# Two DRAINs on GpSimd among the scatters of an attention and mixture-of-experts kernel

## The chip, the cores and the metric

One core of a Trainium2 chip runs one program from its first instruction to its last. The metric is the time of one execution in microseconds on the device (us), taken as the median of three runs. The engines are called as in the profile: PE (TensorE), DVE (VectorE), ACT (ScalarE), POOL (GpSimd) and SP (SyncE). A name with a q behind it (POOLq, SPq) is the engine's queue, where waits on semaphores, branches and DRAINs are recorded.

## The reference, cut to what matters

```python
scores = scale * q @ k.T                        # 8 x 8 heads, 576 x 576, head_dim 64
bias = -(cum[:, :, :, None] - cum[:, :, None, :])     # cum: cumsum of max(s, 0)
scores = where(causal, -1e9, scores + minimum(bias, 0))
attn = exp(scores - max) / (sum + 1e-9)
x = (attn @ v) laid out as 4608 tokens x 512
logits = x @ w_gate + modality_bias[modality_id]      # 8 experts
e_idx = argmax(logits);  gate_w = softmax(logits)[e_idx]
for e in range(8):                              # each token goes to one expert
    h = maximum(x[e_idx == e] @ w1[e], 0)       # 512 -> 1024
    out[e_idx == e] = gate_w * (h @ w2[e])      # 1024 -> 512
```

## The kernel before, in words

The program has two stages. In the attention stage 32 pairs of heads are worked off one after the other. Finished tokens are sorted by expert: each row of a token goes to a list in device memory by an indirect DMA that POOL issues (line L724, 36 of them, of 128 tokens each at most). Besides, POOL splits the queries and keys into a high and a low part in this stage (L323, L327).

The second stage is the expert stage. `M.run` in `build` takes a list of 19 blocks. The first 18 are blocks of 256 tokens of one expert each (`block`, which ends in `second`), the nineteenth takes two quarters of 64 tokens in one go (`two`). Each block loads its tokens and its expert's weights by DMAs on SP, ACT and DVE split the weights into two parts, PE multiplies, and the scaled result `ys` is written to its rows of the output by indirect DMAs that POOL issues, here called scatters: two in each of the 18 blocks (L1067, 128 rows each, the first released by ACT at L1066, the second by DVE at L1064), one in the nineteenth (L1177, 128 rows in two halves from DVE at L1176). `M.last[2]` always holds the scatter that was issued last. From the first of these scatters on POOL has nothing else to do in this stage.

Behind the 19 blocks stands a loop over further quarters (`For_i` at L1355) with a count that is read from the routing (L1353). In the profiled execution its body does not run. Behind the loop each engine waits for the semaphores of all others (rows with L1355), and then comes the end of the program (rows with L1379): a DRAIN on each engine, a meeting of all engines through semaphores that POOL leads, the clearing of the semaphores, and a second meeting.

The order on each engine is that in which a scheduler lets the instructions go; `tc.issue_after(i)` puts the instructions made inside it behind the instruction i on their engine. `finish(k)` is called ahead of block number k, counted from zero, so at its call `M.last[2]` is the last scatter of the k-th block counted from one.

Of the kernel before, what the change touches and what calls it, by code (L numbers as in the profile page):

```python
# [1287 lines left out]
def build(tc, qkv, s, mid, wg, mb, w1, w2, out):  # L1288
    nc = tc.nc
    with ExitStack() as ctx:  # L1290
        dr = ctx.enter_context(tc.tile_pool(name="dr", bufs=1, space=DRAM))
        lists = dr.tile([8 * CAP, ROW], F32, name="lists")
        c = ctx.enter_context(tc.tile_pool(name="const", bufs=1))
        ident = c.tile([P, P], F32, name="ident")
        make_identity(nc, ident)
        R = Route(ctx, tc, lists)
        M = Moe(ctx, tc, R, w1, w2, ident, out)
        xctx = ctx.enter_context(ExitStack())
        pos = []
        with ExitStack() as actx:  # L1300
            xps = [xctx.enter_context(tc.tile_pool(name="xp0", bufs=2, side="right"))]
            A = Attn(actx, tc, qkv, s, ident, wg)

            def newx(bp):
                if bp == 1:
                    A.t1.close()
                    xps.append(xctx.enter_context(tc.tile_pool(name="xp1", bufs=2, side="right")))
                xp = xps[bp % 2]
                return [xp.tile([P, 4, XW // 2, 8, 2], F32, name="x"), xp.tile([P, 4, XW // 2, 8, 2], F32, name="x"),
                        xp.tile([P, 1, XW // 2, 8, 2], F32, name="xq", bufs=1)]  # L1310

            pos.append(lambda: A.xo)

            def done(bp, x):
                def first():
                    yield from R.first()
                    yield from M.early()
                yield from R.group(bp, x, lambda: pos[0](), A.pw_ if bp < 3 else None, (lambda: A.bg.append([first(), False])) if bp == 2 else None)

            setup = {**A.more, 5: A.consts, 14: R.consts, 17: lambda: A.save(0), 26: lambda: A.save(1), 20: lambda: R.setup(mid, mb, A.t1p)}  # L1320
            bg = A.run(32, newx, done, setup)
            assert len(bg) == 1
            for _ in range(NGS):
                next(bg[0][0])
        with ExitStack() as mctx:
            M.open(mctx)
            pos[0] = lambda: M.ps.tile([P, 512], F32, name="rt", bufs=1)

            def routed():
                with ExitStack() as after:  # L1330
                    for i in M.tr:
                        after.enter_context(tc.issue_after(i.ins))
                    after.enter_context(tc.high_priority(offset=PRI2))
                    for _ in bg[0][0]:
                        pass
                xctx.close()
                M.open2(mctx)

            def finish(k):
                if 1 <= k <= 4:  # L1340
                    with ExitStack() as after:
                        for i in (M.hold, M.last[1].ins):
                            after.enter_context(tc.issue_after(i))
                        R.pad((2 * k - 2, 2 * k - 1))
                        if k == 2:
                            for _ in R.rest():
                                pass

            M.run([("t2", b, 2) for b in range(N2)] + [("t3", b, 2) for b in range(N3)] + [("t4", 0, 0)], early=True, then=finish, routed=routed)
            with ExitStack() as after:  # L1350
                for i in [M.hold] + [i.ins for i in M.last]:
                    after.enter_context(tc.issue_after(i))
                n = nc.values_load(R.t4["tot"][0:1, 0:1], min_val=0, max_val=NQ)  # L1353
            M.stop = 1 << 30
            with tc.For_i(NS, n) as i:  # L1355
                M.hold = None
                M.run([("t4", i, 1)])
# [25 lines left out]
```

## Time and profile before

| | us |
|---|---|
| median of three runs | 837.39 (836.03 to 838.33) |
| the profiled execution | 836.2 |
| its span, first to last instruction | 834.4 |
| PE busy in the span | 812.8 (97%) |
| POOL busy in the span | 360.8 (43%) |
| last scatter (L1177) starts | 823.71 |

The span is what the trace shows; the 1.8 us between it and the execution's own time lie outside the records. The views used below are the page, the answers on one line of the kernel (for each operation on each engine: how many, the shortest, the median and the longest duration in ns, and the first and the last start in us), the timeline of POOL (start, duration, engine, line, operation, and in brackets how long the engine sat idle before and what ended that) and a table of the busy time of each engine in chosen stretches.

### The profile page before, as it was taken

How to read it: one execution, taken by the hardware profiler on the slowest of the kernel's cores; microseconds unless marked ns; L12 is line 12 of the kernel's file. 1: busy time of each engine (PE TensorE's matmuls, PEld its weight loads, DVE VectorE, ACT ScalarE, POOL GpSimd, SP SyncE). 2: the span in 40 equal slices, each digit the busy share in tenths (PEclk: the TensorE clock that was granted, in tenths of full speed). 3: DMA queues.
4: the chain of work that ended last, by engine and by line, in shares of the span. 5: the costliest groups of instructions: out<-in, count | busy, mean ns of one | idle time of the engine just before them, and what ended most of it. 6: DMA issues, size and time to landing. Idle time of an engine off the chain costs nothing. (4 is left out here: it accounts for less than half of the span.)

```text
span 834.4 us, 16877 instructions
## 1 busy us (share of the span) xinstructions
PE 812.8 (97%) x5692; PEld 696.1 (83%) x5692; DVE 545.9 (65%) x1502; ACT 541.8 (65%) x1292; POOL 360.8 (43%) x384
## 2 busy tenths in 40 slices
PE   7999999999999999999999999999999999999994
PEld 6778887887888778778988889999988889999872
DVE  6666667666766677767389766555556666555872
ACT  6888888888888888885265555544445555544662
POOL 8959768988688877991410000000000000000110
PEclk9999999999999999999999999999999999999997
DMA  7665555866667656737797866665555566665950
GB/s 234 185 195 179 180 177 185 261 206 193 178 188 227 204 164 198 230 106 268 259 375 257 310 243 255 255 251 204 205 205 205 214 250 255 255 236 208 355 181 3
DMA packets 68549, 182.31 MB, mean 218 GB/s; under 512 B 7993, under 2 KB 8889, under 8 KB 68334
## 3 DMA queue, kind: packets, MB, share of 16 engines
q1 hardware_dynamic: 62622, 161.17, 57.1%
q0 software_dynamic: 5840, 20.06, 6.2%
q8 instruction: 45, 0.74, 0.4%
q14 instruction: 42, 0.34, 0.1%
HBM read 144.73 MB, written 26.80 MB: 206 GB/s over the span
## 5 line engine op out<-in xcount | busy, mean ns | idle before, releaser
L1067 POOL DMA_INDIRECT out<-ys,oi x36 | 36.8, 1023 | 368.1 <-ACT ys L1066 297.5
L397 DVE CUSTOM_DVE_ANT_0 pe<-sp,mk 128x512 f32<-128x512 f32 (+3 forms) x256 | 121.3, 488 | 63.1 <-PE sp L395 58.9
L417 ACT ACTIVATE pe<-pe,mx 128x512 f32<-128x512 f32 (+3 forms) x256 | 143.9, 563 | 21.4 <-DVE mx L397 20.0
L427 PE MATMUL pt<-ident,pe 128*128 128x128 f32 x640 | 118.6, 283 | 3.3 <-ACT PT L430 2.3
L430 ACT COPY PT<-pt 128x512 f32<-128x512 f32 (+3 forms) x256 | 106.6, 417 | 13.7 <-PE pt L427 13.0
L1083 ACT ACTIVATE hT<-hp 128x512 fp32r<-128x512 f32 x72 | 42.9, 595 | 93.0 <-PE hp L1081 92.6
L467 PE MATMUL o<-PT,V 128*64 128x320 f32 (+4 forms) x896 | 100.7, 364 | 0.0
L373 PE MATMUL sp<-KA,QH 128*128 128x256 f32 (+2 forms) x256 | 97.1, 388 | 1.8 <-POOL KA L236 1.8
L427 PEld LDWEIGHTS pt<-ident,pe 128*128 128x128 f32 x640 | 76.0, 142 | 26.3 <-ACT PT L430 10.5
L467 PEld LDWEIGHTS o<-PT,V 128*64 128x64 f32 x896 | 58.6, 136 | 41.0 <-issue 9.2
L1081 PE MATMUL hp<-xT,wcb 128*128 128x256 f32 x648 | 89.6, 282 | 0.0
L395 PE MATMUL sp<-KB,QL 76*128 76x256 f32 (+2 forms) x256 | 88.3, 349 | 1.3 <-DMA QL<-ek 1.3
L1081 PE MATMUL hp<-xT,wca 128*128 128x256 f32 x624 | 87.3, 282 | 0.5 <-ACT xT L1033 0.5
L327 POOL TENSOR_TENSOR KA<-rawk,KA 64x576 fp32r<-64x576 f32 x62 | 86.9, 1418 | 0.2
L327 POOL TENSOR_TENSOR QL<-rawq,QH 64x576 fp32r<-64x576 f32 x62 | 86.7, 1413 | 0.2
L1084 DVE SCALAR_TENSOR_TENSOR hT<-hp,hT 128x512 fp32r<-128x512 f32 x72 | 49.5, 688 | 55.5 <-ACT hT L1083 55.5
L1081 PEld LDWEIGHTS hp<-xT,wcb 128*128 128x128 f32 x648 | 83.1, 188 | 0.6
L1081 PEld LDWEIGHTS hp<-xT,wca 128*128 128x128 f32 x624 | 80.4, 188 | 1.4 <-issue 0.7
L1056 PE MATMUL y<-wcb,hT 128*128 128x512 f32 x336 | 81.2, 398 | 0.0
L1056 PEld LDWEIGHTS y<-wcb,hT 128*128 128x128 f32 x336 | 62.8, 188 | 14.7
L1081 PE MATMUL hp<-xT,wcc 128*128 128x256 f32 x456 | 64.6, 281 | 0.0
L1056 PE MATMUL y<-wca,hT 128*128 128x512 f32 x264 | 63.9, 398 | 0.0
(285 smaller groups left out, 1614.0 us busy)
## 6 DMA issues: line engine op xcount, KB each, us to landing
wrbw<-in_w SPq DMA_DIRECT2D x104, 512.0 KB
wraw<-in_w SPq DMA_DIRECT2D x56, 512.0 KB
rawq<-in_qkv SPq DMA_DIRECT2D x31, 576.0 KB
rawk<-in_qkv SPq DMA_DIRECT2D x31, 576.0 KB
xg<-lists SPq DMA_DIRECT2D x18, 576.0 KB
V<-in_qkv SPq DMA_DIRECT2D x32, 320.0 KB
KB<-KA SPq DMA_DIRECT2D x62, 144.0 KB
lists<-z SPq DMA_DIRECT2D x8, 576.0 KB
```

What stands on the lines that cost most here:

```text
L327: self.last = nc.gpsimd.tensor_tensor(o, i, h, ALU.subtract).ins
L373: self.pe.append(self.nc.tensor.matmul(sp[:, :nn], QH[:, q0:q0 + P], self.KA[u][:, ab, :nn], start=True, stop=False).ins)
L395: self.pe.append(nc.tensor.matmul(sp[:, :nn], QL[:EXT, q0:q0 + P], KB[:EXT, ab, :nn], start=False, stop=True).ins)
L397: ins = nc.vector.tensor_tensor_reduce(out=t[:, :n], in0=sp[:, :n], in1=self.mk[:, 512 - n:512], scale=-0.125, scalar=3.0e38, op0=ALU.add, ...
L417: self.act = nc.scalar.activation(t[:, :n], t[:, :n], AF.Exp, bias=m, scale=-1.0, accum_out=st["sums"][:, o:o + 1]).ins
L427: self.pe.append(nc.tensor.transpose(out=pt[:, P * j:P * j + P], in_=pe[:, P * j:P * j + P], identity=self.ident).ins)
L430: cp(w[:, :, v:v + P], pt[:, :P * (c + 1)].rearrange("p (j q) -> p j q", q=P))
L467: m = nc.tensor.matmul(o[r, f - q0:q1 - q0], V[:, ab, j, :], PT[ab][:, PTS * j + f if j < 4 else PTW - 64:PTS * j + q1 if j < 4 else PTW], ...
L1056: self.last[0] = nc.tensor.matmul(y[u], hT[:, a, f, P * u:P * u + P], W[4 + f // 2][:, c, 512 * (f % 2):512 * (f % 2) + 512], start=f == 0 ...
L1081: nc.tensor.matmul(hp[:, u], W[k][:, a, f:f + P], xT[:, c, k], start=k == 0 and i == 0, stop=k == 3 and i == 2)
L1083: hi = nc.scalar.activation(hs, hp, AF.Relu)
L1084: lo = nc.vector.scalar_tensor_tensor(hT[:, 1, 2 * m:2 * m + 2], hp, 0.0, hs.bitcast(F32), ALU.max, ALU.subtract)
```

## The change

Two DRAIN instructions on POOL are added. The one at k = 10 stands behind the second scatter of the tenth block, the one at k = 18 behind the second scatter of the eighteenth. A DRAIN has no operands. In the built program neither of the two carries a wait on a semaphore or raises one, and nothing else waits for them. Every other instruction of all five engines keeps its place, its waits and its updates: on POOL 16 scatters lie between the two DRAINs, and the only scatter behind the second one is that of the nineteenth block (L1177).

```diff
             def finish(k):
+                if k in (10, 18):
+                    with tc.issue_after(M.last[2].ins):
+                        nc.gpsimd.drain()
                 if 1 <= k <= 4:
                     with ExitStack() as after:
                         for i in (M.hold, M.last[1].ins):
```

## The prediction

> **What bounds the kernel now.** I began with the head of the page and its chain of waits.
>
> ```profile
> span 834.4 us, 16877 instructions
> PE 812.8 (97%) x5692; PEld 696.1 (83%) x5692; DVE 545.9 (65%) x1502; ACT 541.8 (65%) x1292; POOL 360.8 (43%) x384
> ...
> POOL out L1177 0%; POOLq L1353 0%
> ```
>
> PE is busy 97% of the span, so up to the last block PE sets the time, and POOL at 43% does not. The chain of the end, however, hangs on POOL: its last piece is the scatter at L1177. So next I cut the end of the span into stretches (busy time of each engine, clock, DMA share, GB/s).
>
> ```profile
> 815.00:823.70 8.70, 6.93 (x32) 4.57 (x31) 4.24 (x7) 3.09 (x5) 0.00 (x0) 1.00 0.00 0
> 823.70:826.40 2.70, 0.00 (x0) 0.00 (x0) 0.00 (x0) 0.00 (x0) 0.98 (x1) 0.87 0.07 21
> 826.40:827.50 1.10, 0.00 (x0) 0.00 (x0) 0.00 (x0) 0.00 (x0) 0.00 (x0) 0.50 0.00 0
> 827.50:833.60 6.10, 0.00 (x0) 0.00 (x0) 0.00 (x0) 0.00 (x0) 0.00 (x0) 0.50 0.00 0
> 833.60:834.40 0.80, 0.00 (x0) 0.00 (x0) 0.00 (x0) 0.00 (x0) 0.00 (x0) 0.50 0.00 0
> ```
>
> From 823.7 on no engine computes but for one scatter of 0.98 us, and in the 6.10 us from 827.5 to 833.6 nothing is busy and no byte moves. The answer on the end's line, L1379, says what stands there.
>
> ```profile
> L1379 POOLq EVENT_SEMAPHORE  x4: 17/17/17, 833.6 to 834.3; - x4
> L1379 SPq DRAIN  x3: 7/7/13, 827.0 to 833.9; - x3
> L1379 POOLq DRAIN  x3: 45/103/6043, 827.6 to 834.2; - x3
> L1379 ACTq DRAIN  x2: 8/8/8, 827.1 to 833.9; - x2
> L1379 DVEq DRAIN  x2: 10/14/17, 827.3 to 833.9; - x2
> L1379 PEldq DRAIN  x2: 8/8/8, 827.4 to 833.9; - x2
> ```
>
> Four engines pass their first DRAIN in 7 to 17 ns. POOL's three DRAINs take 45, 103 and 6,043 ns. The long one is the first: it starts at 827.6, and POOL's next semaphore event is at 833.6. All engines wait for POOL in this meeting, so these **6.04 us lie on the path that sets the end**, one for one.
>
> **What the long DRAIN may be made of.** The only DRAIN that POOL runs earlier is in the program's head:
>
> ```profile
> L1367 POOLq DRAIN  x1: 173/173/173, 0.4 to 0.4; - x1
> ```
>
> It stands behind four memsets and takes 0.17 us. The two that follow the long one at the end take 0.10 and 0.05 us. So a DRAIN is short when POOL has issued no DMA before it or since the last DRAIN, and the only long one has all of the program's indirect DMAs behind it:
>
> ```profile
> L724 POOL DMA_INDIRECT lists<-x,di x32: 956/1064/1973, 144.0 to 404.6; - x32
> L724 POOL DMA_INDIRECT lists<-xq,di x4: 960/1025/1065, 190.1 to 405.9; - x4
> L1067 POOL DMA_INDIRECT out<-ys,oi x36: 983/983/1442, 407.1 to 810.8; - x36
> L1177 POOL DMA_INDIRECT out<-ys,oi x1: 984/984/984, 823.7 to 823.7; - x1
> DMA to landing us min/median/max: 2.6/2.6/2.6
> ```
>
> That makes 32 + 4 + 36 + 1 = 73. The last landed at 823.71 + 2.6 = 826.3, before the long DRAIN began, so it is not waiting for data. My reading is that POOL keeps something open for each DMA that it issued and settles it in the DRAIN: 6.043 us / 73 = 83 ns for each, an estimate. If so, a DRAIN leaves the next one only what was issued since.
>
> **The change part by part.** Where the two new DRAINs stand is seen in POOL's timeline.
>
> ```profile
> 618.52 0.98 POOL L1067 DMA_INDIRECT out<-ys,oi  x1 [17.98 <-ACT ys L1066]
> 623.24 0.98 POOL L1067 DMA_INDIRECT out<-ys,oi  x1 [3.73 <-DMA out<-ys,oi]
> 642.04 0.98 POOL L1067 DMA_INDIRECT out<-ys,oi  x1 [17.82 <-ACT ys L1066]
> ...
> 810.82 0.98 POOL L1067 DMA_INDIRECT out<-ys,oi  x1 [2.51 <-DMA out<-ys,oi]
> 823.71 0.98 POOL L1177 DMA_INDIRECT out<-ys,oi  x1 [11.91 <-DVEq L1355]
> ```
>
> *First DRAIN.* The tenth block's second scatter ends at 623.24 + 0.98 = 624.22; the next instruction of POOL that does anything starts at 642.04, after 17.82 us of idling, and waits for ACT. Queued behind the DRAIN are only the next scatters. By my reading it settles 36 + 20 = 56 DMAs, 56 x 83 ns = 4.6 us. Bounds: 0.05 us from the shortest DRAIN row, 6.04 us from the longest. If it has to wait for the scatter's landing as well, that adds no more than the longest landing of a scatter:
>
> ```profile
> DMA to landing us min/median/max: 2.7/5.2/7.7
> ```
>
> Even 7.7 + 6.04 = 13.7 us fit into the 17.82. Cost on the path: 0. The cover is ACT's and PE's work on the eleventh block; without it the whole length would count.
>
> *Second DRAIN.* The eighteenth block's second scatter ends at 811.80, and the last one, L1177, starts at 823.71 when DVE's `ys` is ready: 11.91 us of idling. The queue event ahead of L1177 shows when the scatter before it had landed:
>
> ```profile
> L1177 POOLq EVENT_SEMAPHORE  x1: 17/17/17, 813.6 to 813.6; - x1
> ```
>
> So the landing is through at 813.6. The DRAIN settles 16 DMAs, 16 x 83 ns = 1.3 us; at the upper bound, 6.04 us begun at 813.6, it ends at 819.6, 4.1 us ahead of need. Cost on the path: 0 at either bound, covered by PE, ACT and DVE in the nineteenth block.
>
> *Last DRAIN of the program.* One DMA is left, L1177. Lower bound 0.05 us, upper bound 6.04 us, as now. I take the sum of a short DRAIN and one DMA's share, 0.10 + 0.08, rounded to 0.2 us, since the rows for a DRAIN with little behind it (0.05, 0.10, 0.17) are nearest to that case. Gain: 6.04 - 0.2 = 5.84 us, taken as 5.8.
>
> *What else could shrink.* POOL runs one more queue instruction near the end:
>
> ```profile
> L1355 POOLq INC_SWDGE_SEM  x1: 1638/1638/1638, 824.5 to 824.5; - x1
> L1355 POOLq EVENT_SEMAPHORE  x12: 42/43/43, 826.4 to 827.3; - x12
> ```
>
> If its 1.64 us too come from open DMAs, POOL's twelve semaphore waits start sooner, but the fifth of them still has to wait for the landing at 826.3; only four of them, some 0.08 us apart, come forward. That is at most 0.4 us; I put it into the lower end of the range and not into the sum.
>
> **Sum.** Against the profiled execution: 836.2 - 5.8 = 830.4 us (span 834.4 - 5.8 = 828.6, and the same 1.8 us around it). The median of the runs lies 1.2 us above that execution, at 837.39; against it the forecast is 831.6 us, and I write 831.5.
>
> **The rivals.** *First: the 6.04 us stay, time 837.4.* The long part could belong not to the 73 but to whatever stands behind the second new DRAIN: the scatter L1177, the INC_SWDGE_SEM, or a fixed price for a DRAIN after any DMA. Then the two new ones take 6.04 us each under cover, the last takes 6.04 again, and nothing moves. For it: there is one long DRAIN in the trace, and one point cannot tell a price per DMA from a fixed one. Against it: in the head an INC_SWDGE_SEM is followed by a DRAIN of 0.17 us, and one scatter of 128 rows that has landed is little to spend 6 us on.
>
> ```profile
> L1367 POOLq INC_SWDGE_SEM  x1: 31/31/31, 0.2 to 0.2; - x1
> ```
>
> The Trainium skill, GPSIMD Engine Reference, section 2.1 Instruction dispatch, gives such a fixed price: the first call of freshly loaded code pays a load of about 6 us that no instruction shows. By that rule the time stays 837.4. The stretch 827.5 to 833.6 shows a DMA share of 0.00, so no load is seen, though it need not be recorded.
> The Trainium skill, VectorE: DVE Perf Modes, section The DRAIN you can't avoid, calls the DRAINs around a program a constant of about 12 ns on all five engines. By that rule too nothing could be won, and the time stays 837.4. The rows of four engines agree (7 to 17 ns); POOL's 6,043 ns do not.
>
> *Second: a part stays.* If half of the 6.04 is per DMA and half fixed, 3.0 us are won: 834.4. No row speaks for it beyond the same single point.
>
> *Third, on the other side: the scatter behind the second DRAIN gets dearer.* L1177 is on the chain, so each us that its 0.98 grows is a us of the end. If a DRAIN throws out what scatters keep on POOL, and fetching it costs what the long DRAIN costs, L1177 takes 7.0 us and the last DRAIN is as long as before: 837.4 + 6.0 = 843.4. It decides from 2.5 us on if the last DRAIN keeps its 6.04, and from 5.8 us on if it shrinks. Against it: the spread of all 73 issues is 0.96 to 1.97 us, though POOL does other work between them in the first stage.
>
> **How the numbers follow.** Chances: forecast 0.79, the 6.04 us stay 0.13, a part stays 0.04, the scatter gets dearer 0.04. A measurement of this kernel tells about 0.3%, 2.5 us, from no change. Forecast and part-stays are faster: 0.83; no change 0.13; slower 0.04. For the range: around 831.5 the runs of before spread by -1.4 and +0.9; below, the 0.4 us of INC_SWDGE_SEM come on top, which gives 829.7; above, I go to 834.4, the case in which a part stays. That leaves out the first and third rival, 0.17.
>
> **What would show it.** Right: the last stretch of the trace has a POOL DRAIN of under 0.5 us between the semaphores of L1355 and the meeting, the added DRAINs take about 4.6 and 1.3 us (with the landing in front), the scatters after them start at the same distance behind `ys` as now, and PE's time up to 823 is unchanged. Wrong: the DRAIN at the end is still near 6 us (first rival) or 3 us (second), or L1177 takes well over 1 us (third).

## The result, and the profile after

| | before | changed |
|---|---|---|
| median of four runs | 836.71 us (835.80 to 838.33) | 829.38 us (829.02 to 830.96) |
| the profiled execution | 836.2 us | 829.02 us |
| its span | 834.4 us | 827.3 us |
| last scatter (L1177) starts | 823.71 us | 823.07 us |
| POOL's first DRAIN at the end | 6.043 us | 0.128 us |

The changed kernel takes 0.9914 of the time of before, with a 95% interval of 0.9893 to 0.9935: it is faster, by a little under 1%. The forecast was 831.5 us with a range from 829.7 to 834.4. The sign and the mechanism are as forecast; the measured median lies 0.3 us below the range.

In the changed kernel the line of the loop's end is L1358 (L1355 before) and that of the program's end L1382 (L1379 before). The answer on the end's line (operation, count, shortest, median and longest duration in ns, first and last start in us):

```profile
L1382 POOLq EVENT_SEMAPHORE  x4: 17/17/17, 826.5 to 827.2; - x4
L1382 SPq DRAIN  x3: 7/7/13, 826.1 to 826.7; - x3
L1382 POOLq DRAIN  x3: 51/103/128, 826.2 to 827.0; - x3
```

The long DRAIN is gone: 128 ns where it took 6,043. The same answer for the line of the two added DRAINs, and for the end of the loop:

```profile
L1342 POOLq DRAIN  x2: 3655/7172/10688, 622.3 to 810.1; - x2
...
L1358 POOLq EVENT_SEMAPHORE  x12: 42/43/1122, 824.0 to 826.0; - x12
L1358 POOLq INC_SWDGE_SEM  x1: 193/193/193, 823.6 to 823.6; - x1
```

The added DRAINs took 10.69 and 3.66 us. Behind the last scatter, INC_SWDGE_SEM fell from 1,638 to 193 ns. The page's head and the stretches at the end (start and end, length, then busy time of PE, its weight loads, DVE, ACT and POOL, clock, DMA share, GB/s):

```profile
span 827.3 us, 16879 instructions
PE 812.1 (98%) x5692; PEld 695.5 (84%) x5692; DVE 545.6 (66%) x1502; ACT 541.3 (65%) x1292; POOL 360.5 (44%) x384
```

```profile
823.10:825.40 2.30, 0.00 (x0) 0.00 (x0) 0.00 (x0) 0.00 (x0) 0.95 (x1) 0.70 0.07 22
825.40:826.20 0.80, 0.00 (x0) 0.00 (x0) 0.00 (x0) 0.00 (x0) 0.00 (x0) 0.50 0.00 0
826.20:826.50 0.30, 0.00 (x0) 0.00 (x0) 0.00 (x0) 0.00 (x0) 0.00 (x0) 0.50 0.00 0
826.50:827.30 0.80, 0.00 (x0) 0.00 (x0) 0.00 (x0) 0.00 (x0) 0.00 (x0) 0.50 0.00 0
```

Each engine has as many instructions as before, but for the two DRAINs, and its busy time is the same within 0.1%; the empty stretch of 6.10 us at the end became one of 0.3 us. POOL's timeline around the added DRAINs (start, duration, engine, line, operation, idle time before and what ended it):

```profile
622.50 0.98 POOL L1067 DMA_INDIRECT out<-ys,oi  x1 [3.62 <-DVE hT L1084]
641.41 0.98 POOL L1067 DMA_INDIRECT out<-ys,oi  x1 [17.93 <-ACT ys L1066]
...
810.30 0.98 POOL L1067 DMA_INDIRECT out<-ys,oi  x1 [2.52 <-DMA out<-ys,oi]
823.07 0.98 POOL L1177 DMA_INDIRECT out<-ys,oi  x1 [11.78 <-DVEq L1358]
```

The scatters behind both DRAINs still wait for ACT and DVE, after 17.93 and 11.78 us of idling (17.82 and 11.91 before): the DRAINs lie wholly inside that idle time.

The 834.44 - 827.27 = 7.17 us between the two spans divide into pieces:

| piece of the span | before | changed | difference |
|---|---|---|---|
| start to L1177 | 823.71 | 823.07 | -0.64 |
| L1177's start to the start of POOL's first DRAIN at the end | 3.845 | 3.172 | -0.67 |
| that DRAIN | 6.043 | 0.128 | -5.92 |
| the rest (meeting of the engines) | 0.84 | 0.90 | +0.06 |

The first piece is not the change's doing. It stands in the trace by the first of the indirect DMAs to the lists, 480 us ahead of the first added DRAIN:

```profile
L724 POOL DMA_INDIRECT lists<-x,di x32: 959/1064/1973, 143.4 to 404.0; - x32
```

That is 143.4 against 144.0 before, and from there on the two traces stay about as far apart (0.5 to 0.7 us at the scatters shown). In the traces of the runs below, this first start lies anywhere from 143.4 to 146.9 whether or not a DRAIN was added, so one pair of traces cannot be compared closer than some microseconds ahead of L1177; only the pieces behind it can.

### The profile page after: what moved, and what is told of

Same layout as the page of the kernel before. It is cut to its first block, busy times and chain, and to the rows that moved or that the text cites. A ratio compares the mean times of both kernels' runs of the same rounds, so it can differ in the third digit from the quotient of the medians.

```text
span 827.3 us, 16879 instructions
## 1 busy us (share of the span) xinstructions
PE 812.1 (98%) x5692; PEld 695.5 (84%) x5692; DVE 545.6 (66%) x1502; ACT 541.3 (65%) x1292; POOL 360.5 (44%) x384
## 6 DMA issues: line engine op xcount, KB each, us to landing
KB<-KA SPq DMA_DIRECT2D x62, 144.0 KB
```

## The experiments

**Theories.** A: POOL keeps each DMA that it issued open and settles it in its next DRAIN, about 0.083 us each; the DRAIN also waits for the landing of the last scatter (the time at which the trace shows its data arrived). A DMA is called open here when POOL has issued it since its last DRAIN. B: the end's DRAIN has a fixed price (a load of some 6 us, or a price of a DRAIN after any DMA) that a DRAIN somewhere earlier pays once. C: a price per DMA that depends on what else runs, since the first added DRAIN took 10.69 us, not 4.6.

**The changed kernel once more, alone and beside the others.** No edit. It ran in two of the three series.

> The changed kernel itself, unaltered, once more. The theory of open DMAs (POOL's DRAIN settles each DMA that POOL issued since its last DRAIN; the one at the program's end shrinks from 6.04 to about 0.13 us): 0.8% faster than before, some 6.5 to 7 us. The rest of the first result's gain, 0.64 us, was there in the trace before the first added DRAIN ran. If that is chance of the start, the first scatter to the lists starts anywhere between about 143.3 and 144.1 us whatever the kernel, and the gain over many runs is near 6.5 us; if it belongs to the changed kernel, that scatter starts near 143.4 again and the gain is 7.2 us.

Measured: 830.25 us against 836.54 of before, 0.9929 (0.9915 to 0.9943). Its first list DMA starts at 143.4 us again, but so it does with the DRAINs in the head and with the DRAIN behind the last scatter (both below), which gain next to nothing: that start does not belong to the change.

> The changed kernel once more on the chip and in the company of the two others. With a gain of 6.6 us (5.9 from the DRAIN at the end and 0.7 from the shorter INC_SWDGE_SEM and an earlier landing) the ratio lies near 0.992; with 7.3 us as in the first result near 0.991; with 5.8 us, the sum of the prediction, near 0.993. The first scatter to the lists starts anywhere between 143.3 and 147 us by chance.

Measured: 829.31 us against 836.24, 0.9923 (0.9909 to 0.9937). The interval holds all three of the expected ratios, so it does not choose among them. The DRAINs repeat: 10.04 and 10.60 us for the first (it varies with the landing), 3.655 and 3.664 for the second, 128 ns both times at the end. By the three ratios the gain is thus 5.9, 6.4 and 7.2 us.

**Both DRAINs in the program's head**, ahead of POOL's first indirect DMA. If B held in the form of a price of the first DRAIN, it would be paid there; a price of a DRAIN after any DMA is not tested by this kernel.

```diff
-        nc.gpsimd.affine_select(out=self.tri[:, 0], ...
+        tri = nc.gpsimd.affine_select(out=self.tri[:, 0], ...
...
+        for _ in range(2):
+            with self.tc.issue_after(tri.ins):
+                tri = nc.gpsimd.drain()
```

> Both DRAINs stand ahead of the first indirect DMA of the program instead of among the scatters. Open DMAs: each takes 0.05 to 0.2 us, the DRAIN at the end keeps about 6.0 us, no change in time within 0.3%. Rival that two more instructions or any earlier DRAIN is what helps: the DRAIN at the end is short and the time 7 us less. Rival that a DRAIN always costs 6 us once POOL has run any DMA code: same prediction as open DMAs here.

Measured: 835.68 us, 0.9992 (0.9983 to 1.0001). The added DRAINs, the loop's end and the program's end:

```profile
L626 POOLq DRAIN  x2: 41/963/1885, 31.6 to 33.5; - x2
L1358 POOLq INC_SWDGE_SEM  x1: 1644/1644/1644, 823.6 to 823.6; - x1
L1382 POOLq DRAIN  x3: 45/103/6033, 826.7 to 833.3; - x3
```

The end's DRAIN stays at 6,033 ns, and so does the INC_SWDGE_SEM: running a DRAIN before does nothing, it has to stand behind the DMAs. The first one took 1.885 us with no DMA open, which I had not expected: it stood behind POOL work that was queued but not done, the last of which ended at 33.44 us, 0.07 us before the DRAIN did. The second, directly behind it, took 41 ns, the price of a DRAIN with nothing to do. The Trainium skill, PSUM — Partial Sum Buffer, section Engine vs sequencer instructions, says that a drain waits until the engine is fully idle; these two rows agree.

**One DRAIN only, behind the tenth block.**

```diff
-                if k in (10, 18):
+                if k == 10:
```

> Only the DRAIN behind the tenth block; 17 DMAs of POOL follow it. Open DMAs at 83 ns each: the DRAIN at the end takes 17 x 0.083 = 1.4 us, the gain is 4.6 us from it and up to 0.7 us from a shorter INC_SWDGE_SEM and its followers, 5.0 us in all. Fixed price for a DRAIN after any DMA: 6.0 us at the end, no gain. Price by age (only what was issued long ago costs): near 0.1 us at the end, gain as with both.

Measured: 830.59 us, 0.9933 (0.9919 to 0.9946).

```profile
L1342 POOLq DRAIN  x1: 10670/10670/10670, 625.9 to 625.9; - x1
L1358 POOLq INC_SWDGE_SEM  x1: 518/518/518, 827.1 to 827.1; - x1
L1382 POOLq DRAIN  x3: 51/103/1445, 829.8 to 831.8; - x3
```

With 17 DMAs left open (16 and L1177) the end's DRAIN takes 1,445 ns, between the 128 of one and the 6,043 of 73: (1445 - 128) / 16 = 82 ns for each. B falls: a fixed price has no middle. INC_SWDGE_SEM follows too, 518 ns.

**One DRAIN only, behind the eighteenth block.** It meets all 72 open DMAs at once, and C at the first DRAIN's rate would have it at 12 us.

```diff
-                if k in (10, 18):
+                if k == 18:
```

> Only the DRAIN behind the eighteenth block; it finds 72 DMAs open, one follows it. Open DMAs: 0.13 us at the end, as in the changed kernel. The added DRAIN: at the rate of the quiet end 72 x 0.083 = 6.0 us, done at about 817.5, hidden; at the rate of the changed kernel's first DRAIN under load (10.69 - 1.2 = 9.5 us for 56, 0.17 each) 12.2 us, done at about 823.5, so that the last scatter L1177 starts up to 0.5 us late. If instead the 10.69 us were mostly waiting for the landing of the scatter before it, the added DRAIN takes no more than 6 to 7 us here. Time within 0.5 us of the changed kernel.

Measured: 830.06 us, 0.9928 (0.9915 to 0.9942).

```profile
L1342 POOLq DRAIN  x1: 7174/7174/7174, 810.8 to 810.8; - x1
L1382 POOLq DRAIN  x3: 51/103/138, 826.7 to 827.5; - x3
```

```profile
811.03 0.98 POOL L1067 DMA_INDIRECT out<-ys,oi  x1 [2.52 <-DVE hs L1161]
823.50 0.98 POOL L1177 DMA_INDIRECT out<-ys,oi  x1 [11.49 <-DVEq L1358]
```

The record of an added DRAIN begins when the queue reaches it, here 0.2 us before the scatter in front of it even starts. The scatter ends at 811.035 + 0.983 = 812.018, the DRAIN at 810.812 + 7.174 = 817.986: 5.97 us for 72 DMAs, 83 ns each, in the midst of the expert stage. C falls, and a single DRAIN gives the whole gain: it ends 5.5 us before L1177 starts.

**One DRAIN long after its scatter's landing.** The DRAIN of the tenth block moves into the middle of the eleventh, behind a copy of eight numbers on POOL that serves only to hold it there. The 56 open DMAs are the same, but all have landed.

```diff
+            if m == 3 and self.drain:
+                d = nc.gpsimd.tensor_copy(self.my.tile([1, 8], F32, name="dr", bufs=1), hT.bitcast(F32)[:1, 0, 6, :8])
+                with self.tc.issue_after(d.ins):
+                    nc.gpsimd.drain()
...
+                M.drain = k == 10
```

> One DRAIN with 56 DMAs open as the changed kernel's first, but moved 10 us later into the eleventh block, behind a copy of 8 numbers on POOL that waits for ACT, when the scatter before it has landed (the copy is added to make POOL wait and its result is not used). The changed kernel's first DRAIN took 10.69 us and ended 2.36 us behind the landing. If that length was a slower rate under load, 0.17 us for each DMA, this one takes 9.5 us. If it was the landing plus what is left to do behind it, and the rate is 83 ns as at the end, it takes 56 x 0.083 = 4.7 us. The DRAIN at the end, with 17 open, 1.4 us again.

Measured in one run: 828.45 us.

```profile
L1092 POOLq DRAIN  x1: 5442/5442/5442, 630.9 to 630.9; - x1
L1385 POOLq DRAIN  x3: 51/103/1445, 824.5 to 826.4; - x3
```

```profile
630.93 0.74 POOL L1090 COPY dr<-hT 1x8 f32<-1x8 f32 x1 [7.36 <-ACT hT L1084]
```

The copy ends at 631.67, the DRAIN at 630.904 + 5.442 = 636.346: 4.68 us for 56 DMAs, 84 ns each. (The scatter in front had landed at 629.51, before the copy ended.) The answer on the scatter in front of the changed kernel's first DRAIN gives the landing there:

```profile
L1067 POOL DMA_INDIRECT out<-ys,oi x1: 983/983/983, 622.5 to 622.5; - x1
DMA to landing us min/median/max: 8.1/8.1/8.1
```

So the 10.69 us of that DRAIN are the landing and then only a part of the settling: the landing came 8.1 us after the scatter's start, at 630.62, and the DRAIN ended at 632.96, 2.34 us later, not 4.7. In all five traces with a DRAIN directly behind the tenth block and 56 DMAs open this distance is 2.34 us, while the DRAIN itself takes 9.66 to 10.69 us. The settling had partly run while the landing was awaited. This kernel's time, though, was lower than the theory allows for, which led to the two kernels below that have this copy, one without DRAINs and one with the two of the change.

**A DRAIN behind each of the 18 blocks.**

```diff
-                if k in (10, 18):
+                if k:
```

> A DRAIN behind each of the 18 blocks: the first finds 38 DMAs open, the others 2. Two halves (41 ns for each DMA that can be done ahead of the last landing, 41 ns that cannot): each ends at the landing of its scatter + 41 ns x open DMAs + about 0.1 us, so 0.1 to 0.2 us behind the landing with 2 open and 1.7 us with 38. Whole price behind the landing (83 ns for each): 0.2 to 0.3 us and 3.2 us. A fixed part in every DRAIN would show as over 0.5 us behind the landing. End: 0.13 us. Time as the changed kernel within 0.3%, since 8 + 1 us fit into the 18 us between blocks.

Measured: 829.41 us, 0.9917 (0.9900 to 0.9933).

```profile
L1342 POOLq DRAIN  x18: 3077/7208/9330, 413.2 to 810.4; - x18
L1382 POOLq DRAIN  x3: 51/103/128, 826.6 to 827.4; - x3
```

Eighteen DRAINs cost no more than two, though the record shows 3.1 to 9.3 us for each: most of that is the wait for the landing. From the second on, each has two DMAs open and ends 0.12 us behind the landing (the last of the scatter's 16 semaphore updates); the first, with 38 open, 1.61 us behind it.

**More DMAs.** Each of the 36 scatters is followed by a second one that writes its first 64 rows again with the same values; no DRAIN is added. So 109 DMAs are open at the end, and the number of scattered rows grows by a half (that of all rows that POOL's DMAs move, lists included, by a quarter).

```diff
-            self.last[2] = nc.gpsimd.indirect_dma_start(
-                out=self.out, ...ap=oi[:, u:u + 1]..., in_=ys, ...)
+            for n in (P, 64):
+                self.last[2] = nc.gpsimd.indirect_dma_start(
+                    out=self.out, ...ap=oi[:n, u:u + 1]..., in_=ys[:n], ...)
```

> No DRAIN added; each of the 36 scatters of the 18 blocks is followed by one more that writes the first 64 of its 128 rows a second time, so 109 DMAs stand open at the end instead of 73, with 25% more rows. Price for each DMA: the DRAIN at the end takes 109 x 0.083 = 9.0 us and the time grows by 3.0 us. Price for each row: 6.04 x 1.25 = 7.5 us, 1.5 us slower. Fixed price: 6.04 us, no change. INC_SWDGE_SEM: 1.64 us with 73 open, 0.52 with 17, 0.19 with 1, so 20 ns for each and 2.4 us here. The more scatters themselves are hidden.

Measured: 841.27 us, 1.0064 (1.0042 to 1.0085).

```profile
L1356 POOLq INC_SWDGE_SEM  x1: 2347/2347/2347, 826.0 to 826.0; - x1
L1380 POOLq DRAIN  x3: 45/103/8983, 829.8 to 839.3; - x3
```

The DRAIN takes 8,983 ns: (8983 - 6043) / 36 = 82 ns for each DMA more, the same as between 1 and 17. Since a second scatter has only half the rows of the first and yet costs the same, the price is per DMA and not per row. Of the span's growth of 5.2 us the DRAIN explains 2.9; 0.4 more lie in the scatter-to-DRAIN piece (4.245 against 3.845 us, with INC_SWDGE_SEM at 2,347 ns), 0.5 came in the expert stage, most of it in the eighteenth block (0.4), and 1.3 at the start of the program, where no DMA had been added yet. By the medians the growth is 3.5 to 7.1 us; the two terms that follow the count give 3.3 of it, and the rest is open.

**A DRAIN directly behind the last scatter.** This puts the settling of all 73 ahead of the loop's end instead of behind it, beside the landing of L1177.

```diff
+            with tc.issue_after(M.last[2].ins):
+                nc.gpsimd.drain()
```

> One DRAIN directly behind the last scatter L1177, ahead of the semaphore waits of the loop, with 73 open. It is on the path that sets the end. The DRAIN at the end takes 0.05 to 0.1 us. Two halves: the first 3.0 us run from the scatter's end (824.7) and overlap its landing (826.3), the second 3.0 us follow, done at 830.7, then 2 us of load, branch and semaphore waits and 0.9 us of the meeting: 0.5 to 0.9 us faster than before. Whole price behind the landing: done at 832.4, 0.5 to 1 us slower than before. Either way it keeps under 15% of the changed kernel's gain.

Measured: 836.29 us, 0.9999 (0.9989 to 1.0009).

```profile
L1351 POOLq DRAIN  x1: 7266/7266/7266, 822.8 to 822.8; - x1
L1381 POOLq DRAIN  x3: 39/43/103, 832.8 to 833.4; - x3
```

```profile
823.08 0.98 POOL L1177 DMA_INDIRECT out<-ys,oi  x1 [12.03 <-DVEq L1357]
```

The DRAIN ends at 822.84 + 7.27 = 830.11, which is 6.05 us behind the scatter's end at 824.06: on the path, the settling costs what it cost at the end. I had expected 0.5 to 0.9 us from the overlap with the landing. It did not come: POOL's loop count and loop end are queued behind the DRAIN, and from 830.11 to the next DRAIN at 832.77 they took 2.66 us. So it is the idle time of POOL before L1177 that makes the added DRAINs free.

**The copy without a DRAIN.** From the experiment with the late DRAIN, only the copy and its tile of 32 bytes.

```diff
+            if m == 3 and self.drain:
+                nc.gpsimd.tensor_copy(self.my.tile([1, 8], F32, name="dr", bufs=1), hT.bitcast(F32)[:1, 0, 6, :8])
...
+                M.drain = k == 10
```

> The run with the late DRAIN came out at 828.45 us with 17 DMAs left for the end, 1.3 us less settled than in the changed kernel and yet faster: between 385 and 822 us its matmuls pulled ahead of every other kernel of this study by 1.9 us, step by step. It differs from the others in the copy on POOL and in a tile of 32 bytes for it, which moves most tiles of the expert stage up by 32 bytes. This kernel has the copy and the tile but no DRAIN. If the addresses or the copy give the 1.9 us: 0.2% faster than before, a DRAIN of 6.0 us at the end. If it was chance of that one execution, or the late DRAIN's: no change.

Measured: 833.20 us, 0.9966 (0.9952 to 0.9980).

```profile
L1068 POOL DMA_INDIRECT out<-ys,oi x36: 982/983/1438, 406.6 to 808.7; - x36
L1383 POOLq DRAIN  x3: 45/103/6043, 824.6 to 831.2; - x3
```

The end's DRAIN is what it was, and still the kernel is faster: from the first to the last of the 36 scatters it takes 808.7 - 406.6 = 402.1 us, against 810.8 - 407.1 = 403.7 before, and from there to the last scatter (821.07) 12.4 against 12.9. So the late DRAIN's low time came from the copy or its tile, not from the DRAIN.

**The changed kernel with that copy.**

```diff
+                M.drain = k == 10
+                if k in (10, 18):
+                    with tc.issue_after(M.last[2].ins):
+                        nc.gpsimd.drain()
```

> The changed kernel with the same copy and tile. The two add up if the one is the end's DRAIN and the other the stretch from 385 to 822 us: 6.6 + 1.9 = 8.5 us less than before, 1.0%, near 828 us. If the 1.9 us were chance: as the changed kernel, 0.7 to 0.8%.

Measured: 827.94 us, 0.9904 (0.9888 to 0.9919).

```profile
L1346 POOLq DRAIN  x2: 3667/6666/9664, 623.0 to 809.4; - x2
L1386 POOLq DRAIN  x3: 51/103/128, 825.3 to 826.0; - x3
```

The two gains add up only in part: 827.94 against 829.31 for the changed kernel in the same series, 1.4 us, where the copy alone won 3.0 against before. It is the fastest kernel measured in more than one run. Its interval overlaps that of the change alone (0.9909 to 0.9937).

**All DRAINs together.** Rows in which the landing did not hold the DRAIN up. The time is the DRAIN's own record, and for the rows of 56 and 72 it is counted from the end of the POOL instruction in front:

| DMAs open | DRAIN, us | where |
|---|---|---|
| 0 | 0.041 | second DRAIN in the head |
| 1 | 0.128 | end, changed kernel |
| 17 | 1.445 | end, tenth block only |
| 56 | 4.68 | behind the copy in the eleventh block |
| 72 | 5.97 | behind the eighteenth block only |
| 73 | 6.043 | end, before |
| 109 | 8.983 | end, second scatters |

One line fits all of them to 0.04 us: 0.046 us and 0.082 us for each DMA that POOL has issued since its last DRAIN. (The two last DRAINs of the program, with none open, take 0.10 and 0.04 to 0.05 us in every trace.) INC_SWDGE_SEM goes the same way with a smaller slope: 193 ns at 1, 518 at 17, 1,638 at 73, 2,347 at 109, some 0.17 us and 0.020 us each (168 ns with none open behind a DRAIN, but 31 ns in the program's head). Where a scatter was still on its way, the end of the DRAIN lay 0.12, 0.70, 1.61 and 2.34 us behind the landing with 2, 16, 38 and 56 DMAs open, 0.041 us each. So half of the price can run ahead of the landing and half cannot. The DRAIN behind the eighteenth block only, with 72 open, fits this too: its scatter landed 1.7 us behind the scatter's end, before the first half (72 x 0.041 = 3.0 us) was through, so the whole 5.97 us ran from the scatter's end and the landing added nothing. Why there are two halves, no record shows.

## Why the prediction was right or wrong

**What bounds the kernel now: right.** The 6.04 us of POOL's DRAIN lay on the path one for one: 5.92 us came off the DRAIN, and the meeting of the engines behind it moved forward by as much.

**What the long DRAIN is made of: right, with the price.** 83 ns for each DMA was 6.043 / 73 from a single row; the line through seven counts gives 82 ns and a constant of 46 ns. That it goes by DMAs and not by rows was only assumed; the second scatters of half the rows show it.

**First DRAIN, 4.6 us, cost 0: right in what it costs the path, and right in size once the landing is parted from it** (4.68 us measured behind the copy). The 10.69 us of the record were inside the bound of 13.7 that I had worked out for landing and settling one after the other, and inside the 17.9 us of idling. The landing, 8.1 us, came later than the 7.7 us that the bound took for the longest. Half of the settling runs ahead of the landing, so the sum of the two is more than is needed.

**Second DRAIN, 1.3 us, cost 0: right.** 3.66 us with the landing in front; L1177 took 983 ns as before and waited for DVE as before.

**Last DRAIN, 0.2 us, gain 5.84: right.** 0.128 us, gain 5.92.

**What else could shrink: the term that I sized at 0.4 us and left out of the sum.** It came, and by the way that I had described. INC_SWDGE_SEM fell by 1.45 us, and four of the twelve semaphore waits came forward: in the changed kernel the fifth lasts 1,122 ns, until the landing. The stretch from L1177's start to the end's DRAIN fell from 3.845 to 3.172 us. Of these 0.67 us, 0.31 belong to the one trace of before: there POOL's queue reached INC_SWDGE_SEM 0.81 us behind L1177's start (824.51), against 0.49 us in the changed kernel (823.56) and 0.49 to 0.50 in the other traces without a DRAIN directly behind L1177. Two other traces with 73 DMAs open have 3.54 and 3.53 us for the stretch, and all with 1 or 17 open 3.16 to 3.17, so 0.36 us belong to the open DMAs: the bound of 0.4 was nearly the value. A cost that scales with the same thing as the main term, and whose bound is as small as this one, belongs in the sum by its likely value.

**The sum: its base was too high, and it lacked the term of the last paragraph.** This is the step that put the range wrong. I took the forecast from the median of three runs, 837.39, "1.2 us above that execution", rather than from the profiled execution at 836.2. With a fourth run the median of before is 836.71, and in the three later series of 9 to 15 runs 836.14 to 836.54: the base was 0.7 to 1.2 us high. With the 0.36 left out that is 1.0 to 1.6 of the 2.1 us by which the forecast missed; what the rest is stays open. From the profiled execution and with that term the sum would have been 836.2 - 5.9 - 0.4 = 829.9 us. The two terms give 6.3 us in all, which lies inside the intervals of all three comparisons of the changed kernel with before (5.4 to 9.0, 4.8 to 7.1 and 5.3 to 7.6 us); the remainder of the first one's 7.3 is within what such a comparison can tell. The lower end of the range took the runs' spread and the 0.4 us, but not that the base itself, a median of three, was uncertain by 1 us. Of the changed kernel's three medians, 829.38 and 829.31 lie below the range and 830.25 lies in it.

**First rival (the 6.04 us stay): falls** by the 128 ns of the changed kernel, where L1177 and INC_SWDGE_SEM still stand behind the second DRAIN, and by the 1,445 ns at 17 open DMAs. Of the rule of a fixed load on the first call (the Trainium skill, GPSIMD Engine Reference, section 2.1 Instruction dispatch) no sign is seen in these DRAINs: 0.128, 1.445, 6.043 and 8.983 us for the same instruction at the same place are no fixed price. Nor is POOL's DRAIN a constant of about 12 ns, as the Trainium skill, VectorE: DVE Perf Modes, section The DRAIN you can't avoid, has it for all five engines: the other four lie near it in every trace here (7 to 17 ns at the end's line), POOL does not, and the measurement decides.

**Second rival (a part stays): falls.** The fixed part is 46 ns, not 3 us.

**Third rival (the scatter behind a DRAIN gets dearer): falls.** L1177 takes 983 ns; behind a DRAIN in each of 18 blocks the time is the same as behind two.

## What to carry to other kernels

In this kernel the DRAIN at the program's end costs 0.082 us for each DMA that POOL has issued, on the path, with nothing to see in the busy shares. Look for it where POOL issues many. One DRAIN on POOL in an idle stretch shortly before the end, long enough for the last landing and the settling, took nearly all of that off here. It has to be idle time: the same DRAIN right behind the last DMA won nothing. An effect that appears only once is found by counting what lies behind it, then tested by changing the count.

## What the runs showed that I had not expected

A tile of 32 bytes and a copy of eight numbers into it brought the kernel to 0.9966 (0.9952 to 0.9980) of its time. The copy itself runs at 630 us, and the lead over before grows gradually, from 0.5 us at the first scatter (406.6 against 407.1) to 1.7 us at the nineteenth (616.80 against 618.52), ahead of the copy, and 2.1 at the 36th. So it is not the copy. In the built program the tile moves hT, xT, the gathered tokens and the weight buffer wcb up by 32 bytes, and leaves wca, wcc and ys where they were; the order of the instructions on all engines is otherwise the same. PE's groups from 500 to 780 us, by form, of before and of the kernel with the copy (busy us and mean ns of one, then idle time):

```profile
L1056 PE MATMUL y<-wcc,hT 128*128 128x512 f32 x183 | 44.1, 397 | 0.0
L1056 PE MATMUL y<-wca,hT 128*128 128x512 f32 x156 | 37.7, 398 | 0.0
```

```profile
L1057 PE MATMUL y<-wcc,hT 128*128 128x512 f32 x180 | 42.4, 392 | 0.0
L1057 PE MATMUL y<-wca,hT 128*128 128x512 f32 x156 | 37.5, 396 | 0.0
```

The second product takes 392 ns in place of 397 on one weight buffer and 396 in place of 398 on another: 183 x 5 + 156 x 2 = 1.2 us in this stretch. All three traces with the tile show 392 and 396 ns, all ten without it 397 and 398. On the third weight buffer, wcb, which moved together with hT, the product takes 398 ns with and without the tile. That fits a cause in the addresses but does not show it: no run moved a tile without the copy, and why an address should matter to these products stays open.

The two halves of the DRAIN's price (0.041 us for each DMA before the landing, 0.041 behind it) and the growth of INC_SWDGE_SEM by 0.020 us for each open DMA were not in my reading either; that a DRAIN also waits for POOL work queued before it (1.885 us in the head) shows only where POOL has such work.
